# Attention scores as three fp32r products of high and low parts, with a new order of a turn's steps

## The chip, the cores and the metric

The kernel runs on one core of a Trainium2 chip. The metric is the device time of one execution in microseconds (us), the median of several runs. A core has five engines that run side by side, each through its own list of instructions in order: TensorE (PE, its weight loads shown as PEld), VectorE (DVE), ScalarE (ACT), GpSimd (POOL) and SyncE (SP, which issues most of the transfers). They wait for one another by semaphores. TensorE reads its operands from the on-chip memory SBUF and writes its results to PSUM, from where VectorE and ScalarE fetch them.

## The reference, cut to what matters

Attention over 8 batches of 8 heads, 576 tokens, 64 channels a head, with a mask by blocks of 64 tokens; then a mixture of 8 experts, of which each token takes one.

```python
def _attn_ref(q, k, v):
    scores = scale * np.matmul(q, k.transpose(0, 1, 3, 2))       # scale = 1/8
    mask = block_i >= block_j                                     # blocks of 64
    scores = np.where(mask, scores, -1000000000.0)
    scores = scores - np.max(scores, axis=-1, keepdims=True)
    attn = np.exp(scores)
    attn = attn / (np.sum(attn, axis=-1, keepdims=True) + 1e-09)
    return np.matmul(attn, v).astype(np.float32)

def _moe_ref(x, w_gate, w1, w2):
    expert_idx = np.argmax(x @ w_gate, axis=1)
    ...
        ye = np.maximum(xe @ w1[e], 0.0) @ w2[e]
        out[mask] = gate_w[mask, None] * ye
```

## The kernel before

**Two stages.** The attention with the router runs first, to about 380 us of the profile; the experts follow. Only the attention is touched. The experts' matmuls already work in fp32r, a float32 format that keeps a part of the mantissa: each factor is split into a high part and the rest, and three products (high by high, low by high, high by low) are summed in PSUM.

**Units.** Two heads make a unit m, 32 in all. The two heads' channels lie in the two halves of the 128 partitions, so a matmul on rows 0 to 63 is the first head's (tiles xa, ya), one on rows 64 to 127 the second's (xb, yb). The 576 queries are cut into a tile 0 of 64 rows and tiles 1 to 4 of 128 rows. Tile i meets 64 + 128 i keys.

**Steps of a unit.** The steps have names, and the number after a colon in the table ORDER is the lag: step X:3 in turn t works on unit t - 3.
- ld loads q (qd), k (kd) and v on SP's queue; pQ scales q by 1/8 (GpSimd, and VectorE for unit 0).
- S0 to S4 are the scores of the tiles, on TensorE: S0 one fp32 matmul of 128 rows for both heads, S1 (192 columns a head), S2 (320), S3 (448), S4 (2 x 288) one fp32 matmul a head on 64 rows. An fp32 matmul shows as two records in the profile.
- K sets the masked corner (VectorE), M takes the row maximum (VectorE), E the exp with its row sum (ScalarE); A and B are the two heads.
- T transposes exps (TensorE, four 128x128 at a time: Ta1, Ta2, Tb1, Tb2, Tk0, Tx3; Tt0 for tile 0), H copies the result to SBUF (@A ScalarE, @D VectorE), V0 to V5 multiply with v (TensorE, two heads in the two 64-column halves of the array), O and O0 copy the output to SBUF.
- F1, F2, F0 transpose the output and give the router's products (TensorE), X and Y scale them (VectorE) with R1 and R2 (one over the sums); Z scales tile 0 (GpSimd).
- z and y run one step of the router of a finished batch, or of what is postponed.

**What sets the order.** `run` goes through ORDER once a turn and issues each step, so ORDER alone fixes each engine's list. There is no planner at run time.

**Buffers.** The scores have two pairs of PSUM banks, "sa" and "sb": S4 (xa, xb) and S1 to S3 (ya, yb) of a unit, and then the next unit, take turns in them, so S4 of a unit waits for the exps E1 to E3 of the unit before, and S1 to S3 wait for E4. The transposes have two banks "pt" in turn. S0, V5 and F1 share a bank "o2", and F2 and F0 the next use of the same bank, so F2 waits for the readers of F1. The output of V has one bank "o".

Of the kernel before, what the change touches and what calls it, by code (L numbers as in the profile page):

```python
# [38 lines left out]
class Attention:  # L39
# [8 lines left out]
    def __init__(self, ctx, tc, ident, qT, kT, vt, w_gate, ends, po):  # L48
        self.tc, self.nc = tc, tc.nc
        self.qT, self.kT, self.vt = qT, kT, vt  # L50
        self.po = po

        self.ends = ends.rearrange("p (i c) -> p i c", c=P)
        self.M = qT.shape[0] * H // 2
        nc = self.nc
        cp = ctx.enter_context(tc.tile_pool(name="acst", bufs=1))
        self.raw = ctx.enter_context(tc.tile_pool(name="araw", bufs=3))
        self.rawv = ctx.enter_context(tc.tile_pool(name="arawv", bufs=5))
        self.spl = ctx.enter_context(tc.tile_pool(name="aspl", bufs=2))
# [32 lines left out]
    def op_ld(self, m):  # L92

        nc = self.nc
        b = m // 4
        qd = self.raw.tile([P, QS], F32, tag="qd", name=f"qd{m}")
        kd = self.raw.tile([P, S], F32, tag="kd", name=f"kd{m}")
        v = self.rawv.tile([P, VS, D], F32, tag="v", name=f"v{m}")
        nc.sync.dma_start(qd, self.qT[b, m % 4])
        nc.sync.dma_start(kd, self.kT[b, m % 4])  # L100
        nc.sync.dma_start(v, self.vt[b, m % 4])
        self.raws[m] = (qd, kd, v)

# [58 lines left out]
    def op_S(self, m, i):  # L162

        mm = self.nc.tensor.matmul
        q, k = self.qs[m], self.raws[m][1]
        if i == 0:
            mm(self.part(1, m, "S0", 432, 496), q[:, 512:], self.raws[m][0][:, 512 + P :], start=True, stop=True)  # L167
            return
        e = 64 + 128 * i
        for c in range(2 if i == 4 else 1):  # L170
            for j in range(2):
                out, _ = self.region(m, i, j)
                if i == 4:
                    out = out[:, c]
                n = out.shape[-1]
                o = (0 if j else S - e) + n * c
                r = slice(64 * j, 64 * j + 64)
                ins = mm(  # L178
                    out, q[r, 128 * (i - 1) : 128 * i], k[r, o : o + n], start=True, stop=True, skip_group_check=True
                )  # L180
                self.uses(m, i, j, ins)
# [187 lines left out]
    def run(self, order, sink, part, other, then, loaded):  # L369

        order = [(name, int(lag)) for name, lag in (x.split(":") for x in order.split())]
        last = max(lag for name, lag in order if name[0] not in "yz")
        left = [20] * (self.M // 4)
        more, pace, asks = iter(()), 1, None

        ends = {  # L380
            "F1": ("F2", "F0"), "X1": ("X2", "Y0@D"), "Y1": ("Y2",), "F2": ("F1",), "X2": ("X1",), "Y2": ("Y1",),
            "F0": (), "Y0@D": (),
        }
        for turn in range(self.M + last):
            if turn == self.M + last - 1:
                order = [(x, lag) for name, lag in order for x in ends.get(name, (name,))]
            for name, lag in order:
                m = turn - lag
                if name[0] == "z":
                    for _ in range(pace):  # L390
                        if asks is None:
                            asks = next(more, None)
                    continue
                if name[0] == "y":
                    other()
# [12 lines left out]
                if name[0] in "XY":
                    left[m // 4] -= 1
                    if left[m // 4] == 5:  # L410
                        part(m // 4, self.xs[m // 4][0])
                    if left[m // 4] == 0:
                        assert asks is None and next(more, "end") == "end"
                        (more, pace), asks = sink(m // 4, *self.xs.pop(m // 4)), None
        while asks != "end":
            if asks == "bank":
                next(then, None)
                asks = more.send(self.ps_t.tile([P, 512], F32, tag="pt", name="bank")[:, 0 : 6 * E])
            else:
# [12 lines left out]

# [889 lines left out]
```

## Time and profile before

| | |
|---|---|
| median of 3 runs | 861.1 us (860.74 to 861.51) |
| the profiled execution's own time | 863.59 us |
| its span, first to last instruction | 861.8 us |
| TensorE busy | 835.7 us (97%), mean granted clock 0.993 |
| ScalarE, VectorE, GpSimd busy over the span | 458.6, 397.9, 395.6 us |
| lines of the score products, busy | 58.3 us for ya, 58.3 us for yb, 41.6 us each for xa and xb, in pairs at the same time |

A row of the timeline gives start, duration, engine, line, operation, output <- inputs, shape and how many instructions were merged into the row (x4). A matmul's duration runs until its last result is in PSUM, so a matmul overlaps the next one; what one costs in a row of them is the distance of the starts. A row that starts after a change of the array's shape starts with its weight load. "[1.43 <-DVE neg L194]" is idle time of the engine before the row and who ended it.

### The profile page before, as it was taken

Reading aid. Unit: us, or ns where it says so; the run is one execution under the profiler, and the core shown is the slowest. Engines: PE = TensorE matmul, PEld = TensorE weight load, DVE = VectorE, ACT = ScalarE, POOL = GpSimd, SP = SyncE. Lnnn points to the kernel's source line nnn. Section 1 sums busy time; section 2 is a strip of 40 time slices with the busy share of each in tenths; the row PEclk is TensorE's granted clock in tenths of the full one; section 3 lists DMA queues with packets and bytes.
Section 4 is the critical chain, followed back from the end, with each engine's and each line's share of the span. In section 5 each row is a group of like instructions: output and inputs, shape, how many; then the busy total and the mean of one; then the engine's idle time right before and its main releaser. Section 6 shows DMA issues by size and latency. Waiting matters only on the chain.

```text
span 861.8 us, 15862 instructions
## 1 busy us (share of the span) xinstructions
PE 835.7 (97%) x4936; PEld 631.1 (73%) x4936; DVE 397.9 (46%) x1145; ACT 458.6 (53%) x1154; POOL 395.6 (46%) x389
## 2 busy tenths in 40 slices
PE   6999999999999999989999999999999999999993
PEld 4666666666666666657888888888888888888882
DVE  4667776777776777658505200047356451000000
ACT  5777777777777777724434443444344334433431
POOL 3222333333444624255845544456656565445451
PEclk9999999999999999999999999999999999999997
DMA  5234638363626355324713411045536431111110
GB/s 197 97 119 157 148 121 162 102 162 96 163 96 151 108 121 176 88 61 172 240 50 123 147 50 43 32 147 178 185 133 238 148 110 38 49 50 37 38 51 28
DMA packets 45687, 99.33 MB, mean 115 GB/s; under 512 B 7585, under 2 KB 10913, under 8 KB 45602
## 3 DMA queue, kind: packets, MB, share of 16 engines
q1 hardware_dynamic: 38082, 78.26, 31.0%
q0 software_dynamic: 7520, 19.97, 7.0%
q8 instruction: 49, 0.80, 0.4%
q14 instruction: 36, 0.29, 0.1%
HBM read 76.76 MB, written 21.98 MB: 115 GB/s over the span
## 4 chain that ended last, share of the span: by engine, by line
PE 93%; ACT 2%; issue 1%; DVE 1%; POOL 1%; another core or an unknown queue 0%; DMA 0%; POOLq 0%; DVEq 0%; ACTq 0%
PE py L987 24%; PE o L903 12%; PE ph L903 12%; PE o L279 11%; PE ya L178 6%; PE xa L178 4%; PE pt L947 4%; PE o L314 3%; PE px L862 2%; PE o L308 1%; ACT pb L209 1%; PE o L167 1%; DVE rc L691 0%; PE sb L1289 0%
## 5 line engine op out<-in xcount | busy, mean ns | idle before, releaser
L987 PE MATMUL py<-w,low 128*128 (+1 forms) x912 | 229.9, 401 | 0.2 <-issue 0.2
L987 PEld LDWEIGHTS py<-w,low 128*128 128x128 f32 x912 | 166.3, 189 | 33.9 <-issue 0.6
L108 POOL TENSOR_SCALAR q<-qd 128x640 f32<-128x640 f32 x31 | 56.1, 1811 | 188.6 <-PE o L167 108.2
L1111 DVE CAST w<-raw 128x1024 fp32r<-128x1024 f32 x60 | 49.4, 873 | 191.1 <-PE o L903 139.6
L967 POOL TENSOR_TENSOR low<-hf,low 128x512 fp32r<-128x512 f32 x72 | 100.5, 1396 | 34.9 <-ACT hf L961 34.9
L881 POOL TENSOR_TENSOR xl<-xf,xh 128x512 fp32r<-128x512 f32 x38 | 50.8, 1338 | 90.2 <-ACT xf L875 90.1
L1117 DVE TENSOR_TENSOR w<-raw,w 128x1024 fp32r<-128x1024 f32 x60 | 80.4, 1400 | 0.0
L957 ACT CAST low<-pt 128x512 fp32r<-128x512 f32 x76 | 45.7, 602 | 57.4 <-PE pt L947 56.1
L903 PE MATMUL o<-w,xh 128*128 x280 | 75.5, 392 | 0.0
L903 PE MATMUL ph<-w,xh 128*128 x280 | 75.4, 391 | 0.0
L209 ACT ACTIVATE pb<-ya,neg 128x320 f32<-128x320 f32 (+2 forms) x93 | 48.5, 525 | 45.5 <-DVE neg L194 45.4
L1010 POOL DMA_INDIRECT out<-y,idx x35 | 40.6, 1161 | 64.0 <-ACT y L1004 64.0
L939 ACT ACTIVATE h<-o 128x512 f32<-128x512 f32 x37 | 22.2, 599 | 74.1 <-PE o L903 74.1
L903 PEld LDWEIGHTS ph<-w,xh 128*128 128x128 f32 x280 | 52.6, 188 | 11.8
L903 PEld LDWEIGHTS o<-w,xh 128*128 128x128 f32 x280 | 52.6, 188 | 11.6
L1004 ACT ACTIVATE y<-py,xg 128x512 f32<-128x512 f32 x38 | 26.2, 689 | 64.3 <-PE py L987 64.3
L939 ACT ACTIVATE h<-ph 128x512 f32<-128x512 f32 x37 | 22.2, 600 | 71.7 <-PE ph L903 71.7
L178 PE MATMUL yb<-kd,q 64*128 64x192 f32 (+1 forms) x186 | 58.3, 447 | 0.0
L178 PE MATMUL ya<-kd,q 64*128 64x192 f32 (+1 forms) x186 | 58.3, 447 | 0.0
L698 POOL DMA_INDIRECT tab<-toks,posi x40 | 41.8, 1044 | 25.1 <-DVE run L665 12.8
L961 ACT COPY hf<-pt 128x512 f32<-128x512 f32 x76 | 46.3, 609 | 10.2 <-POOL low L967 9.2
L844 POOL DMA_INDIRECT xg<-xd,idx x37 | 44.5, 1202 | 10.8 <-POOL idx L840 10.6
(963 smaller groups left out, 1828.8 us busy)
## 6 DMA issues: line engine op xcount, KB each, us to landing
raw<-w SPq DMA_DIRECT2D x60, 512.0 KB, 5.2
qd<-qT SPq DMA_DIRECT2D x32, 352.0 KB
v<-vt SPq DMA_DIRECT2D x32, 352.0 KB
kd<-kT SPq DMA_DIRECT2D x32, 288.0 KB
xd<-xt SPq DMA_DIRECT2D x7, 1026.0 KB
xd<-xg SPq DMA_DIRECT2D x9, 256.5 KB
xg<-w SPq DMA_DIRECT2D x8, 256.0 KB
xd<-x SPq DMA_DIRECT2D x8, 128.0 KB
```

What stands on the lines that cost most here:

```text
L108: engine.tensor_scalar(q, self.raws[m][0][:, 0 : 512 + P], 0.125, None, ALU.mult)
L178: ins = mm(out, q[r, 128 * (i - 1) : 128 * i], k[r, o : o + n], start=True, stop=True, skip_group_check=True)
L209: ins = self.nc.scalar.activation(dst, src, AF.Exp, bias=self.neg[m][:, c : c + 1], scale=1.0, accum_out=self.sums[m][:, c : c + 1])
L279: self.nc.tensor.matmul(out[r], self.raws[m][2][:, slot], self.ph[m, bank][:, c0:c1], start=t in (0, 5), stop=t in (4, 5), skip_group_chec ...
L881: pool.tensor_sub(self.xl, self.xf, self.xh).then_inc(sem["xp"], 1)
L903: m = pe.matmul(self.ph[f], x[:, P * k : P * k + P], weights(k, f, part), start=start and k == 0, stop=stop and k == 3,)
L957: act.copy(self.hh[t % 2][:, f], self.pt[f]).then_inc(sem["ha"], 1)
L961: act.copy(self.hf, self.pt[f]).then_inc(sem["ha"], 1)
L967: engine.tensor_sub(self.hl[t % 2][:, f], self.hf, self.hh[t % 2][:, f]).then_inc(sem["hp"], 1)
L987: m = pe.matmul(self.py[t % 2], h[:, c // 4, P * (c % 4) : P * (c % 4) + P], wf[:, bass.ds(off + (base + 512 * c), 512)], start=n == 0, st ...
L1111: dve.tensor_copy(hi, raw[m % nr]).then_inc(sem["wh"], 1)
L1117: dve.tensor_sub(lo, raw[m % nr], hi).then_inc(sem["wd"], 1)
```

## The change

Tiles 1 to 4 of the scores are computed from a high part and the rest in fp32r. Four steps take the place of pQ: cQ and cK (ScalarE) write the high parts qh = q/8 and kh = k rounded to fp32r, lQ (VectorE) the rest ql = q/8 - qh, lK (GpSimd; VectorE for unit 0) the rest kl = k - kh; q0 (GpSimd) scales tile 0's queries, whose S0 stays in fp32. Each fp32 matmul of S1 to S4 becomes three fp32r matmuls, qh by kh, qh by kl and ql by kh, added up in PSUM, and each of the three runs for the two heads in turn. kd has a pool of its own with two buffers instead of three. ORDER is another one, and in the first turn of lag 3 S0, M0 and E0 of unit 0 come behind E1B.

```diff
+        self.rawk = ctx.enter_context(tc.tile_pool(name="arawk", bufs=2))
...
-        kd = self.raw.tile([P, S], F32, tag="kd", name=f"kd{m}")
+        kd = self.rawk.tile([P, S], F32, tag="kd", name=f"kd{m}")
...
-    def op_pQ(self, m):
-
-        q = self.qs[m] = self.spl.tile([P, 512 + P], F32, tag="q", name=f"q{m}")
+    def half(self, m, k, n, dt=F32R):
+        t = self.qs.setdefault(m, {})[k] = self.spl.tile([P, n], dt, tag=k, name=f"{k}{m}")
+        return t
+
+    def op_cQ(self, m):
+
+        self.nc.scalar.activation(self.half(m, "qh", 512), self.raws[m][0][:, 0:512], AF.Copy, scale=0.125)
+
+    def op_cK(self, m):
+        self.nc.scalar.copy(self.half(m, "kh", S), self.raws[m][1])
+
+    def op_lQ(self, m):
+        self.nc.vector.scalar_tensor_tensor(
+            self.half(m, "ql", 512), self.raws[m][0][:, 0:512], 0.125, self.qs[m]["qh"], ALU.mult, ALU.subtract
+        )
+
+    def op_lK(self, m):
         engine = self.nc.gpsimd if m else self.nc.vector
-        engine.tensor_scalar(q, self.raws[m][0][:, 0 : 512 + P], 0.125, None, ALU.mult)
+        engine.tensor_sub(self.half(m, "kl", S), self.raws[m][1], self.qs[m]["kh"])
+
+    def op_q0(self, m):
+
+        self.nc.gpsimd.tensor_scalar(self.half(m, "q0", P, F32), self.raws[m][0][:, 512 : 512 + P], 0.125, None, ALU.mult)
...
-            for j in range(2):
...
+            for n, (x, y) in enumerate((("qh", "kh"), ("qh", "kl"), ("ql", "kh"))):
+                for j in range(2):
...
+                    ins = mm(
+                        out, q[x][r, 128 * (i - 1) : 128 * i], q[y][r, o : o + w], start=n == 0, stop=n == 2,
+                        skip_group_check=True,
+                    )
...
+            if turn == first:
+
+                turns = [x for x in order if x[0] not in ("M0", "E0")]
+                n = turns.index(("E1B", turn)) + 1
+                turns[n:n] = [(x, turn) for x in ("S0", "M0", "E0")]
+            else:
+                turns = [x for x in order if x[0] != "S0" or turn > x[1]]
...
 ORDER = """
-E3B:3 V5:4 z2:0 O0@D:4 ld:0 Ta1:3 O@A:4 Ha1@A:3 S0:3 S4:2 z6:0 M0:3 Tb1:3 Tk0:3 pQ:1 K4B:2 E0:3 R1:3 K4A:2 z1:0 M4B:2
...
+E2A:3 M0:3 V4:4 M1B:3 ld:0 Ta2:3 M2B:3 z2:0 z3:0 E1A:3 z5:0 Ta1:3 O@D:4 E0:3 E2B:3 z6:0 E1B:3 Ha2@D:3 R1:3 cK:1 F1:4
...
```

What the new ORDER does to the engines' lists is shown at three places. The rows give line, operation, output <- inputs and columns; x2 merges equal rows. In the names xa, xb, ya, yb are the scores, pt the transposes, o the output of V, o21 and o22 the shared small bank (S0 reads qd, V5 reads h0 or v, F reads fold and oT), and a name's first number is the unit.

TensorE from the last transposes of a unit to the V matmuls, before (unit 4's V, unit 5's scores; L245 is Tt0, L178 the scores, L279 V0 and V2):

```order
L248 MATMUL pt4x3_849<-ident_68,pb4_683 128x128 x4
L245 MATMUL pt4t0_854<-ident_68,p04_684 64x128
L178 MATMUL ya5_858<-kd5_510,q5_674 128x192
L178 MATMUL yb5_860<-kd5_510,q5_674 128x192
L178 MATMUL ya5_858<-kd5_510,q5_674 128x320
L178 MATMUL yb5_860<-kd5_510,q5_674 128x320
L178 MATMUL ya5_858<-kd5_510,q5_674 128x448
L178 MATMUL yb5_860<-kd5_510,q5_674 128x448
L279 MATMUL o4_877<-ph4k0_828,v4_377 64x512 x2
```

TensorE around the same steps, after (unit 3's Tt0 and V0, then the first four of S3's six rows of unit 4):

```order
L266 MATMUL pt3t0_838<-ident_68,p03_676 64x128
L300 MATMUL o3_841<-ph3k0_829,v3_290 64x512 x2
L198 MATMUL ya4_848<-kh4_624,qh4_634 128x448
L198 MATMUL yb4_850<-kh4_624,qh4_634 128x448
L198 MATMUL ya4_848<-kl4_789,qh4_634 128x448
L198 MATMUL yb4_850<-kl4_789,qh4_634 128x448
```

and where the scores end, after (the last of S1, then S0, Tx3, Tb1, V5, V2, V3):

```order
L198 MATMUL ya4_848<-kh4_624,ql4_711 128x192
L198 MATMUL yb4_850<-kh4_624,ql4_711 128x192
L186 MATMUL o214_873<-qd4_436,q04_820 128x64
L269 MATMUL pt3x3_882<-ident_68,pb3_675 128x128 x4
L269 MATMUL pt3b1_887<-ident_68,pb3_675 128x128 x4
L300 MATMUL o214_873<-h01_135,v3_290 64x64 x2
L300 MATMUL o3_841<-ph3a2_781,v3_290 64x384
L300 MATMUL o3_841<-ph3b2_856,v3_290 64x384
L300 MATMUL o3_841<-ph3x3_898,v3_290 64x256 x2
```

V0 stands alone ahead of the scores, which run from S3 to S1 now, and S0 with two groups of transposes stands between them and the other V matmuls; before, all V matmuls followed the scores in one group, and S0 stood ahead of S4.

TensorE at the end of V and the start of S4, before (V4, V5, Ta1, S0, S4):

```order
L279 MATMUL o3_742<-ph3a2_714,v3_259 64x128
L279 MATMUL o3_742<-ph3b2_711,v3_259 64x128
L279 MATMUL o213_767<-h01_132,v3_259 64x64 x2
L248 MATMUL pt4a1_779<-ident_68,pb4_683 128x128 x4
L167 MATMUL o213_767<-qd4_375,q4_542 128x64
L178 MATMUL xa5_789<-kd5_510,q5_674 128x288
L178 MATMUL xb5_791<-kd5_510,q5_674 128x288
```

and after (V4, Ta2, Ta1, F1, the first rows of S4):

```order
L300 MATMUL o3_841<-ph3a2_781,v3_290 64x128
L300 MATMUL o3_841<-ph3b2_856,v3_290 64x128
L269 MATMUL pt4a2_924<-ident_68,pb4_835 128x128 x4
L269 MATMUL pt4a1_931<-ident_68,pb4_835 128x128 x4
L335 MATMUL o214_873<-fold_138,oT3_936 128x144 x2
L198 MATMUL xa5_956<-kh5_784,qh5_794 128x288
L198 MATMUL xb5_958<-kh5_784,qh5_794 128x288
L198 MATMUL xa5_956<-kl5_949,qh5_794 128x288
```

F1, which reads the copy oT of the bank that V4 ends, stands two groups behind V4 and ahead of S4; before, it stood behind S4, Tb1 and Tk0.

ScalarE from the exps of tiles 1 to 3 on, before (L209 exps, L286 O, L260 H):

```order
L209 ACTIVATE pb5_815,sums5_812<-ya5_858,neg5_813 128x320
L209 ACTIVATE pb5_815,sums5_812<-yb5_860,neg5_813 128x192
L209 ACTIVATE pb5_815,sums5_812<-ya5_858,neg5_813 128x448
L209 ACTIVATE pb5_815,sums5_812<-ya5_858,neg5_813 128x192
L209 ACTIVATE pb5_815,sums5_812<-yb5_860,neg5_813 128x320
L209 ACTIVATE pb5_815,sums5_812<-yb5_860,neg5_813 128x448
L286 COPY oT4_922<-o4_877 128x512
L260 COPY ph5a1_924<-pt5a1_917 128x512
```

and after (L281 H, L230 exps, L114 cK, L111 cQ):

```order
L281 COPY ph3x3_898<-pt3x3_882 128x512
L281 COPY ph3b1_904<-pt3b1_887 128x512
L230 ACTIVATE pb4_835,sums4_832<-ya4_848,neg4_833 128x448
L230 ACTIVATE pb4_835,sums4_832<-ya4_848,neg4_833 128x320
L230 ACTIVATE pb4_835,sums4_832<-ya4_848,neg4_833 128x192
L230 ACTIVATE p04_836,sums4_832<-o214_873,neg4_833 128x64
L230 ACTIVATE pb4_835,sums4_832<-yb4_850,neg4_833 128x320
L230 ACTIVATE pb4_835,sums4_832<-yb4_850,neg4_833 128x192
L114 CAST kh6_944<-kd6_758 128x576
L281 COPY ph4a1_951<-pt4a1_931 128x512
L111 ACTIVATE qh6_954<-qd6_757 128x512
```

O has left ScalarE for VectorE, cK and cQ have come, and Hx3 and Hb1 stand ahead of E3A, E2A, E1A, E0, E2B and E1B, the readers of the banks that S4 of the next unit writes.

## Rows read from the trace of the kernel before

**Rows 1.** Windows, attention: length, busy us of PE, PEld, DVE, ACT, POOL; clock, DMA.

```profile
25.36:349.62 324.26, 323.75 (x2392) 216.29 (x2392) 231.43 (x884) 242.98 (x734) 117.05 (x111) 1.00 0.49 132
```

**Rows 2.** Timeline, TensorE, one turn: start, us, engine, line, out<-in, columns, merged count.

```profile
58.67 0.51 PE L178 MATMUL xa<-kd,q 64*128 64x288 f32 x1
...
59.50 0.40 PE L178 MATMUL xa<-kd,q 64*128 64x288 f32 x1
...
60.33 0.60 PE L248 MATMUL pt4k<-ident,pb 128*128 128x128 f32 x4
60.77 0.66 PE L314 MATMUL o<-fold,oT 128*128 128x144 f32 x4
...
62.15 0.71 PE L314 MATMUL o<-fold,oT 128*128 128x144 f32 x4
62.79 0.46 PE L308 MATMUL o<-fold,oT 128*64 128x144 f32 x2
...
63.67 0.27 PE L245 MATMUL pt4t<-ident,p 128*64 128x128 f32 x1
...
64.84 0.54 PE L178 MATMUL ya<-kd,q 64*128 64x448 f32 x1
...
65.22 0.54 PE L178 MATMUL ya<-kd,q 64*128 64x448 f32 x1
...
66.60 0.49 PE L279 MATMUL o<-ph4a,v 128*64 128x384 f32 x1
...
69.73 0.51 PE L178 MATMUL xa<-kd,q 64*128 64x288 f32 x1
```

**Rows 3.** Timeline, TensorE's weight loads in the same turn.

```profile
58.67 0.18 PEld L178 LDWEIGHTS xa<-kd,q 64*128 64x128 f32 x1
58.67 0.18 PEld L178 LDWEIGHTS xb<-kd,q 64*128 64x128 f32 x1
58.78 0.19 PEld L178 LDWEIGHTS xa<-kd,q 64*128 64x128 f32 x1
...
63.98 0.19 PEld L178 LDWEIGHTS ya<-kd,q 64*128 64x128 f32 x1
```

**Rows 4.** Timeline, TensorE, the experts: first row of six groups of fp32r, and the row behind them.

```profile
434.02 1.08 PE L903 MATMUL ph<-w,xh 128*128 x4
...
439.52 0.60 PE L862 MATMUL px<-ident,xg 128*128 128x128 f32 x4
```

**Rows 5.** Timeline, ScalarE, the same turn.

```profile
60.53 0.59 ACT L260 COPY ph4b<-pt4b 128x512 f32<-128x512 f32 x1 [0.94 <-PE pt4b L248]
61.02 0.59 ACT L260 COPY ph4k<-pt4k 128x512 f32<-128x512 f32 x1
...
66.16 0.53 ACT L209 ACTIVATE pb<-ya,neg 128x320 f32<-128x320 f32 x1 [1.43 <-DVE neg L194]
...
69.25 0.60 ACT L286 COPY oT<-o 128x512 f32<-128x512 f32 x1
```

**Rows 6.** Timeline, VectorE's copy of 512 columns, and the last V4, O and F.

```profile
62.57 0.68 DVE L260 COPY ph4b<-pt4b 128x512 f32<-128x512 f32 x1
...
368.13 0.27 PE L279 MATMUL o<-ph31b,v 128*64 128x128 f32 x1
...
368.45 0.59 ACT L286 COPY oT<-o 128x512 f32<-128x512 f32 x1 [2.43 <-issue]
...
369.09 0.76 PE L314 MATMUL o<-fold,oT 128*128 128x144 f32 x4 [0.57 <-ACT oT L286]
```

**Rows 7.** Page, costliest groups: count, busy us, mean ns, idle before.

```profile
L108 POOL TENSOR_SCALAR q<-qd 128x640 f32<-128x640 f32 x31 | 56.1, 1811 | 188.6 <-PE o L167 108.2
...
L967 POOL TENSOR_TENSOR low<-hf,low 128x512 fp32r<-128x512 f32 x72 | 100.5, 1396 | 34.9 <-ACT hf L961 34.9
```

**Rows 8.** Timeline, the start.

```profile
3.85 0.77 DVE L108 TENSOR_SCALAR q<-qd 128x640 f32<-128x640 f32 x1 [2.24 <-DMA qd<-qT]
...
4.81 0.81 PE L178 MATMUL xa<-kd,q 64*128 64x288 f32 x1 [4.81 <-DVE fill L485]
```

More of the change, by code (lines that the diff above doesn't have):

```diff
@@ L164, in op_S @@
         mm = self.nc.tensor.matmul
-        q, k = self.qs[m], self.raws[m][1]
+        q = self.qs[m]
         if i == 0:
-            mm(self.part(1, m, "S0", 432, 496), q[:, 512:], self.raws[m][0][:, 512 + P :], start=True, stop=True)
+            mm(self.part(1, m, "S0", 432, 496), q["q0"], self.raws[m][0][:, 512 + P :], start=True, stop=True)
             return
@@ L170, in op_S @@
         for c in range(2 if i == 4 else 1):
-            for j in range(2):
[L172 to L181, printed above, removed]
+            for n, (x, y) in enumerate((("qh", "kh"), ("qh", "kl"), ("ql", "kh"))):
+                for j in range(2):
+                    out, _ = self.region(m, i, j)
+                    if i == 4:
+                        out = out[:, c]
+                    w = out.shape[-1]
+                    o = (0 if j else S - e) + w * c
+                    r = slice(64 * j, 64 * j + 64)
+                    ins = mm(
+                        out, q[x][r, 128 * (i - 1) : 128 * i], q[y][r, o : o + w], start=n == 0, stop=n == 2,
+                        skip_group_check=True,
+                    )
+                    self.uses(m, i, j, ins)
     def op_K(self, m, i, j):
@@ L341, in step @@
         k = name[0]
-        if name in ("ld", "pQ", "R1", "R2", "Z"):
+        if name in ("ld", "cQ", "cK", "lQ", "lK", "q0", "R1", "R2", "Z"):
             getattr(self, "op_" + name)(m)
@@ L378, in run @@
         more, pace, asks = iter(()), 1, None
+        first = dict(order)["E1B"]
         ends = {
@@ L384, in run @@
         for turn in range(self.M + last):
+            if turn == first:
[4 more added lines that the diff above has]
+                turns = [x for x in order if x[0] != "S0" or turn > x[1]]
             if turn == self.M + last - 1:
-                order = [(x, lag) for name, lag in order for x in ends.get(name, (name,))]
-            for name, lag in order:
+                turns = [(x, lag) for name, lag in order for x in ends.get(name, (name,))]
+            for name, lag in turns:
                 m = turn - lag
@@ L425 @@
 ORDER = """
-E3B:3 V5:4 z2:0 O0@D:4 ld:0 Ta1:3 O@A:4 Ha1@A:3 S0:3 S4:2 z6:0 M0:3 Tb1:3 Tk0:3 pQ:1 K4B:2 E0:3 R1:3 K4A:2 z1:0 M4B:2
-R2:3 F1:4 Hb1@A:3 Ta2:3 Hk0@A:3 X1:4 Y1:4 M4A:2 Tb2:3 F2:4 E4B:2 y0:0 Z:3 Hb2@D:3 F0:4 Ha2@A:3 Y2:4 z4:0 Tx3:3 Tt0:3
-E4A:2 X2:4 S1:2 z5:0 z0:0 z3:0 Ht0@A:3 Y0@D:4 S2:2 K1A:2 K2A:2 S3:2 K1B:2 Hx3@A:3 K2B:2 V0:3 V2:3 M2A:2 K3A:2 M1B:2
-M3A:2 E2A:2 E1B:2 V1:3 y1:0 E3A:2 V3:3 M1A:2 K3B:2 M2B:2 E1A:2 M3B:2 V4:3 E2B:2
+E2A:3 M0:3 V4:4 M1B:3 ld:0 Ta2:3 M2B:3 z2:0 z3:0 E1A:3 z5:0 Ta1:3 O@D:4 E0:3 E2B:3 z6:0 E1B:3 Ha2@D:3 R1:3 cK:1 F1:4
+X1:4 lK:2 Ha1@A:3 Y1:4 cQ:1 S4:2 Tk0:3 z1:0 Tb2:3 q0:2 y0:0 R2:3 F2:4 K4A:2 F0:4 Z:3 Hk0@A:3 K4B:2 M4A:2 Tt0:3 M4B:2
+V0:3 X2:4 E4A:2 Y0@D:4 E4B:2 z4:0 S3:2 Hb2@A:3 Y2:4 S2:2 S1:2 lQ:1 S0:2 z0:0 K3B:2 K3A:2 M3B:2 K1A:2 K2A:2 M3A:2 M1A:2
+Tx3:3 Tb1:3 Ht0@A:3 M2A:2 y1:0 V5:3 E3B:2 K1B:2 Hx3@A:3 V2:3 O0@D:3 Hb1@A:3 V3:3 E3A:2 V1:3 K2B:2
 """
```

## The prediction

> **What bounds the kernel now.** I read the page first, where TensorE is the one engine that is busy nearly throughout, then the view by windows for the attention part [rows 1]: between the first S4 matmul of unit 2 and that of unit 31, 29 turns, TensorE is busy in 323.75 of 324.26 us, ScalarE in 242.98 and VectorE in 231.43, at a granted clock of 1.00. A turn is 324.26/29 = 11.18 us, and one without extra router work 69.73 - 58.67 = 11.06 [rows 2]. So TensorE's own list of work sets the turn; the other engines have 8.38 (ScalarE), 7.98 (VectorE) and 4.04 us (GpSimd) of work in it. The expert stage after it isn't touched. Only what shortens TensorE's list, and no wait in its place, will move the end.
>
> "Busy" hides dead time, though. In the timeline of one turn [rows 2] the columns stream back to back inside a group, but between groups that use the array in different shapes (full, 64-row halves for S, 64-column halves for V and F0) nothing streams for a while. S4's last pair starts at 59.50 and takes 0.24, so it ends at 59.74; the transposes behind it take 0.109 each (four in 60.77 - 60.33) and must have begun at 59.90, since the next group starts at 60.33: **0.16 us dead**. Tt0 (one transpose, 63.67) ends at 63.78, the first S1 columns run at 63.98, when the first weights are in and the next load begins [rows 3]: **0.20**. S3 ends at 65.22 + 0.38 = 65.60, and V0, two times 0.43 before 66.60, begins at 65.74: **0.14**. Seven such changes stand in a turn.
>
> **The products.** An fp32 matmul is two records, each 0.83 ns a column: S4 4 x 0.24 (59.50 - 58.78 is three of them), S1 and S2 64.84 - 63.98 = 0.86, S3 2 x 0.38: 2.58 us a unit for both heads, which run side by side [rows 2, 3]. After it there are three fp32r matmuls in place of two records, 15 pairs instead of 10. The only fp32r rate in the trace is that of the experts: 24 matmuls of 512 columns from 434.02 to 439.52 [rows 4], 0.229 us each. That is 0.016 over the 0.213 that 512 columns would take at half of a record's 0.83 ns, and one size doesn't tell whether the excess grows with the columns. A pair can't follow the last sooner than a weight load: 58.78 - 58.67 = 0.11, the two halves at once [rows 3].
> - Excess by column (0.447 ns): S1 3 x 0.11, S2 3 x 0.143, S3 3 x 0.200, S4 6 x 0.129 = 2.13; gain 0.45.
> - Excess fixed at 0.016: 0.33 + 3 x 0.149 + 3 x 0.203 + 6 x 0.136 = 2.21; gain 0.37.
> - No excess: 0.33 + 3 x 0.135 + 3 x 0.187 + 6 x 0.12 = 2.02; gain 0.56.
>
> I take 0.41, between the first two, because both keep to the one row there is. 64-row fp32r isn't in the trace at all; the bound above is that the halves don't overlap (a rival below).
>
> The Trainium skill (TensorE: Matmul & The Clock Gate, Back-to-back issue gap) gives N/2.4 + 2.5 ns for a warm matmul, 216 ns at 512 columns. The experts' rows differ, with 229, so the rows stand in the sum; by the page the gain would be near the third line, a rival below.
>
> **The new order's changes of shape.** This is the part that speaks against it. V0 moves out of the V group to before S3, and S0 with two transposes comes between S1 and V5. Where a turn had Tt0|S1 and S3|V0 (0.20 + 0.14 = 0.34) it has Tt0|V0 (0.15, like S3|V0), V0|S3 (0.20), S1|S0 (0.20, since a 128-column load stands open as at Tt0|S1) and Tb1|V5 (0.15): 0.70. The others change their neighbours, not their kind; F0|Tt0 in place of F0|Tx3 loads half the weights and gives 0.03 back. Nine changes instead of seven, **+0.33 us**, between 0.28 and 0.37. So four fifths of what the products give go here.
>
> **Waits.** In this turn F2 should begin at 62.15 and, counted back from F0 at 62.79 (a gap of 0.20 less the load of 0.11, and four records of 144 columns, 0.12 each), begins at 62.22: it waits 0.07 for VectorE's X1 and Y1, which stand right behind F1. Now S4, Tk0 and Tb2 stand between F1 and F2, so that goes: -0.07, a little more in turns like those that make the mean 11.18. In its place F1 stands close behind V4: V4 ends, VectorE's copy O starts 0.21 later, takes 0.68 as a copy of 512 columns does there, the load comes 0.05 after it and takes 0.11: 1.05 us [rows 6]. Meanwhile TensorE does a change (0.16), Ta2 and Ta1 (0.87): 1.03. So F1 waits +0.02; 0 to 0.1. What next is late is S4, which needs the exps of the unit before out of its banks (third rival).
>
> **What lies beside.** ScalarE gets cQ and cK (a 512-column copy starts 61.02 - 60.53 = 0.49 after another there [rows 5], so 0.49 + 0.55) and gives O (0.47) away: 8.38 to 8.95. VectorE gets lQ and O (0.68 each): 7.98 to 9.34. GpSimd gives pQ away (1.81) for lK (1.396 x 576/512 = 1.57) and q0 (128 of pQ's 640 columns, 0.36) [rows 7]: 4.04 to 4.16. All lie under TensorE's 10.9, and cost nothing as long as that holds; VectorE is now at 85%, which is where the cover is thinnest. kd has two buffers instead of three: its load waits on SP's queue until lK has read the unit two before, with the v load and the router's row transfers queued behind it. Its reader cK comes a turn later, some 10 us, so 0.
>
> **Start and end.** The first S4 begins at 4.81, after VectorE's pQ at 3.85 [rows 8]. Now cK and cQ must run on ScalarE, then lQ and lK on VectorE before the second product: 0.55 + 0.49 + 0.68 + 0.76 = 2.5 from 3.85 to 4.8, so the second product comes at 6.3 to 7.3. S streams less in that stretch too. I put +1.0, between 0 and +2. The drain keeps its length: 0.
>
> **Sum.** -0.41 + 0.33 - 0.07 + 0.02 = -0.13 us a turn, 30 turns: -3.9; with the start -2.9. The profiled execution took 863.59 for its span of 861.8, 2.5 more than the runs' median 861.1; on it the sum gives 860.7, on the median **858.2 us**. With the ends of the gain (0.37, 0.45) and of the changes, 855 to 859.4.
>
> **Rivals.**
> - *The products run at full rate*: gain 0.56, 0.15 x 30 = 4.4 less, **853.8**. For it: fp32 records of the same shape show no excess (0.24 for 288 columns is 0.83 ns each). Against: every fp32r row has it. 0.11.
> - *The changes eat it all*: gain 0.37, changes 0.37, F1 waits 0.10: -0.37 + 0.37 - 0.07 + 0.10 = +0.03 a turn, +0.9, and the start between 0 and +1: **862**. It takes only the upper end of three terms, none of them far. 0.22.
> - *Slower: S4 waits for ScalarE.* S4 writes the banks that the exps of the unit before read. From the end of Tb1, ScalarE needs 0.20 to its copy (in the rows Tb1 ends at 60.33, its copy starts at 60.53), 0.49 for Hb1, then E3A, E2A, E1A, E2B, E1B (six exps take 69.25 - 66.16 = 3.09, less one of 448 columns, about 0.61: 2.48 [rows 5]), E0 taken as 0.49 and 0.05 to TensorE: 3.71. TensorE has in between, by columns at 0.83 ns and two records, V5 0.11, V2 0.64, V3 0.43, V1 0.85, V4 0.21, then Ta2 and Ta1 0.87, F1 0.48, and changes of 0.15, 0.16 and 0.09: 3.99. It decides from 0.28 more on ScalarE's chain, one maximum of VectorE that comes late; each 0.1 beyond costs 3.0 us. At 0.54 more: -0.13 + 0.26 = +0.13 a turn, +3.9 + 1.0, **866**. For it: ScalarE already starts its exps only after 1.43 us of idling for a maximum [rows 5], and VectorE gets 17% more work. 0.22.
> - *The halves don't run side by side in fp32r*, so the change doesn't do what it says: some 2 x 2.1 = 4.2 instead of 2.17, +2.0 x 30 on the forecast, **919**. Against: the fp32 halves load their weights in the same 0.11 [rows 3]. 0.03.
>
> **How the numbers follow.** The forecast has 0.42. A difference under 0.2% (1.7 us, 859.4 to 862.8) is about what a measurement of this kernel can tell from none. Faster: 0.42 + 0.11 = 0.53; same 0.22; slower 0.22 + 0.03 = 0.25. The likeliest's own range is 855 to 859.4. From 851.5 to 866 the range holds all of the forecast, the second case, most of the first and half of the third: about 0.84.
>
> **What would show it.** Right: pairs of 288 columns 0.13 apart, 448 0.20, 192 0.11; nine gaps of 0.15 to 0.20 in a turn; turns of 10.93; no idle time before S4. Wrong: pairs 0.12 apart (first rival); turns of 11.05 to 11.1 with the gaps larger or F1 waiting 0.1 (second); TensorE waiting before S4 for ScalarE's exps, or before a V matmul for its copy (third); the second half of a pair starting when the first ends (fourth).

## The result, and the profile after

The changed kernel takes **867.97 us** (median of 7 runs, 866.55 to 869.24) against 861.49 for the kernel before (7 runs, 860.74 to 864.37): ratio **1.0074**, 95% interval 1.0064 to 1.0085. It is slower by 6.5 us. The forecast was 858.2, and its range ended at 866. What follows is read from one profiled execution of each kernel. That of the kernel before took 2.5 us more than the median of its runs, that of the changed one 1.3 more, so the spans differ by 5.5 where the medians differ by 6.5.

The page of the changed kernel, head and busy times (engine, busy us, share, instructions). TensorE has 2.6 us less work than before and VectorE 51 us more, in a span that is 5.5 us longer:

```profile
span 867.3 us, 16704 instructions
## 1 busy us (share of the span) xinstructions
PE 833.1 (96%) x5256; PEld 644.7 (74%) x5256; DVE 449.3 (52%) x1209; ACT 471.3 (54%) x1186; POOL 402.4 (46%) x421
```

The view by windows of the changed kernel, first S4 matmul of unit 2 to that of unit 31, answers to [rows 1]: 327.34 us instead of 324.26, and TensorE idles 5.9 of them instead of 0.5.

```profile
core 0: us, PE busy (x) PEld busy (x) DVE busy (x) ACT busy (x) POOL busy (x), PEclk, DMA share, GB/s
27.90:355.24 327.34, 321.46 (x2688) 227.24 (x2688) 276.43 (x942) 254.11 (x762) 124.85 (x140) 1.00 0.48 128
```

Three stretches make up the 5.5: S4 of unit 2 starts 2.54 later (27.90 against 25.36), the 29 turns take 3.08 more, and from S4 of unit 31 to the end there is 0.12 less.

The products run as forecast. TensorE's timeline of the changed kernel at an undisturbed S4 and at the start of the next: from the second pair on, pairs of 288 columns follow each other at 0.13, both halves at once.

```profile
231.18 0.40 PE L198 MATMUL xa<-kh,qh 64*128 64x288 f32 x1
...
231.42 0.29 PE L198 MATMUL xa<-kl,qh 64*128 64x288 f32 x1
231.43 0.29 PE L198 MATMUL xb<-kl,qh 64*128 64x288 f32 x1
231.56 0.29 PE L198 MATMUL xa<-kh,ql 64*128 64x288 f32 x1
231.69 0.29 PE L198 MATMUL xa<-kh,qh 64*128 64x288 f32 x1
...
242.16 0.39 PE L198 MATMUL xa<-kh,qh 64*128 64x288 f32 x1
```

From 231.18 to 242.16 are 10.98; the turns without router work take 10.96 to 10.98, called a **clean turn of 10.97** here (11.06 before, 10.93 forecast). But in most batches of four units one turn takes 11.4, and in four of them the next takes 12.2 to 12.5. They are turns with the router's work. TensorE's waits of the changed kernel in that stretch, as far as they are longer than the 0.15 that the view counts (waiting instruction <- what released it: us in all, times, longest), are of these three kinds; the third stands four times, once in each of the four long turns:

```profile
PE o L335 <- ACT pb L230: 2.2, 6, 0.7
PE o L186 <- PE yb L198: 2.1, 4, 0.8
PE o L300 <- ACT ph17x L281: 0.4, 1, 0.4
```

**The long turn.** VectorE and GpSimd of the changed kernel, in the turn whose S4 starts at 207.66:

```profile
211.01 0.29 DVE L351 COPY x<-o 64x144 f32<-64x144 f32 x1
211.22 2.77 DVE L623 TENSOR_TENSOR oh<-cd,w 128x40 bf16<-128x40 f32 x1
213.91 0.18 DVE L354 TENSOR_TENSOR lg<-o,rs 128x32 f32<-128x32 f32 x1
214.01 0.67 DVE L117 SCALAR_TENSOR_TENSOR ql<-qd,qh 128x512 fp32r<-128x512 f32 x1
214.70 0.11 DVE L210 MEMSET yb<- 64x64 f32 x1
...
210.75 1.43 POOL L123 TENSOR_TENSOR kl<-kd,kh 128x576 fp32r<-128x576 f32 x1
212.13 0.56 POOL L127 TENSOR_SCALAR q<-qd 128x128 f32<-128x128 f32 x1
212.63 1.29 POOL L1267 TENSOR_TENSOR high<-xg,zero 128x512 fp32r<-128x512 f32 x1
```

The router's step oh has 40 columns, and takes 0.18 and 0.20 in the two batches where GpSimd idles beside it. Here it takes 2.77: it ends when GpSimd has finished lK, q0 and the weight split. In three batches it takes 2.44 to 2.46 (the same three steps). In the last two, without a split behind q0, it takes 0.70 and 0.71, and ends 0.07 behind lK, while q0 still runs. What stands behind it on VectorE is late: Y2, for which S0 waits (for the bank), and ql, then the maxima of S3, for which ScalarE waits, and then V3 for ScalarE's copy:

```profile
215.50 0.63 ACT L230 ACTIVATE pb<-yb,neg 128x448 f32<-128x448 f32 x1 [3.50 <-DVE neg L215]
...
214.19 0.41 PE L186 MATMUL o<-qd,q 128*128 128x64 f32 x2 [0.77 <-PE yb L198]
...
216.76 0.65 PE L300 MATMUL o<-ph17x,v 128*64 128x256 f32 x4 [0.36 <-ACT ph17x L281]
```

The Trainium skill (SBUF — State Buffer, "SBUF: two separate sides") says that VectorE and GpSimd share one pair of SBUF ports as an exclusive lock: a VectorE step with two SBUF inputs and a GpSimd step that reads SBUF don't run at once. The trace agrees in that oh takes 0.70 instead of 0.18 and ends right behind lK; that it was not let in between the three steps, here and in three other batches, goes beyond what is said there.

**The turn ahead of it.** VectorE and TensorE of the changed kernel, in the turn before (S4 at 196.24). VectorE's ql takes 1.56, as lK runs beside it until 200.91, and from there to O VectorE has no pause. At the end three router steps (z2, z3, z5) stand ahead of O. V4 ends at 205.5, O starts at 206.17, and F1 waits.

```profile
199.89 1.56 DVE L117 SCALAR_TENSOR_TENSOR ql<-qd,qh 128x512 fp32r<-128x512 f32 x1
...
201.64 0.11 DVE L210 MEMSET yb<- 64x64 f32 x1
...
205.10 0.61 DVE L607 TENSOR_REDUCE L<-lg 128x32 f32<-128x256 f32 x1
205.82 0.20 DVE L610 TENSOR_REDUCE m<-L 128x5 f32<-128x40 f32 x1
206.05 0.20 DVE L612 TENSOR_TENSOR L<-L,m 128x40 f32<-128x40 f32 x1
206.17 0.68 DVE L307 COPY oT<-o 128x512 f32<-128x512 f32 x1
...
207.00 0.73 PE L335 MATMUL o<-fold,oT 128*128 128x144 f32 x4 [0.31 <-ACT pb L230]
```

The view names ScalarE's pb as what released F1, but that had long been done; what came last is O (206.17 + 0.68 = 206.85, and the load). In all five turns of this kind (11.41 to 11.43) ql takes 1.56. How much is the hold of ql and how much the three steps, b_z4_lq tells below.

### The profile page after: what moved, and what is told of

Read it like the earlier page. It is cut to its first block, busy times and chain, and to the rows that moved or that the text cites. A ratio compares the mean times of both kernels' runs of the same rounds, so it can differ in the third digit from the quotient of the medians.

```text
span 867.3 us, 16704 instructions
## 1 busy us (share of the span) xinstructions
PE 833.1 (96%) x5256; PEld 644.7 (74%) x5256; DVE 449.3 (52%) x1209; ACT 471.3 (54%) x1186; POOL 402.4 (46%) x421
## 4 chain that ended last, share of the span: by engine, by line
PE 87%; DVE 5%; ACT 4%; issue 2%; DMA 0%; POOL 0%; SPq 0%; POOLq 0%; DVEq 0%; ACTq 0%
PE py L1016 25%; PE ph L932 12%; PE o L932 12%; PE o L300 9%; PE o L335 4%; PE pt L976 4%; PE ya L198 4%; PE xa L198 3%; ACT pb L230 2%; PE px L891 2%; DVE neg L215 2%; PE o L329 1%; DVE ql L117 1%; PE o L186 1%; DVE oh L623 1%
## 5 line engine op out<-in xcount | busy, mean ns | idle before, releaser
L1140 DVE CAST w<-raw 128x1024 fp32r<-128x1024 f32 x60 | 47.4, 841 | 189.0 <-PE o L932 136.3
L243 POOL TENSOR_SCALAR p<-p,rs 128x64 f32<-128x64 f32 x32 | 14.1, 442 | 199.1 <-DVE rs L239 138.0
L1146 DVE TENSOR_TENSOR w<-raw,w 128x1024 fp32r<-128x1024 f32 x60 | 83.8, 1454 | 0.0
L230 ACT ACTIVATE pb<-yb,neg 128x448 f32<-128x448 f32 (+2 forms) x93 | 49.7, 550 | 57.6 <-DVE neg L215 53.9
L932 PEld LDWEIGHTS ph<-w,xh 128*128 128x128 f32 x280 | 52.6, 188 | 11.8
L727 POOL DMA_INDIRECT tab<-toks,posi x40 | 43.6, 1089 | 32.3 <-DVE lg L354 13.3
L230 ACT ACTIVATE pb<-ya,neg 128x448 f32<-128x448 f32 (+2 forms) x93 | 48.4, 544 | 0.0
L335 PE MATMUL o<-fold,oT 128*128 128x144 f32 x256 | 44.4, 296 | 3.5 <-ACT pb L230 2.2
```

The costliest lines, as they stand in the source:

```text
L230: ins = self.nc.scalar.activation(dst, src, AF.Exp, bias=self.neg[m][:, c : c + 1], scale=1.0, accum_out=self.sums[m][:, c : c + 1])
L335: mm(t[:, i], self.oT[m, 0][:, o : o + P], w, start=True, stop=True)
L932: m = pe.matmul(self.ph[f], x[:, P * k : P * k + P], weights(k, f, part), start=start and k == 0, stop=stop and k == 3,)
L1140: dve.tensor_copy(hi, raw[m % nr]).then_inc(sem["wh"], 1)
L1146: dve.tensor_sub(lo, raw[m % nr], hi).then_inc(sem["wd"], 1)
```

## Experiments

**Theory**: the change cuts TensorE's list as forecast, but GpSimd's new steps lK and q0 lie beside VectorE's, and each holds the other (stretches it while it runs). **Rivals**: VectorE simply has too much work in the router's turns; or the products or the order cost more than read.

Starts of S4, from TensorE's timeline of each profiled execution (29 turns from S4 of unit 2 to that of unit 31; the next column is the rest of the span), and medians beside the kernel before on the same chip:

| kernel | S4 of unit 2 | clean turn | 29 turns | last S4 to end | median us | ratio to before (95%) |
|---|---|---|---|---|---|---|
| before | 25.36 | 11.06 | 324.26 | 512.2 | 861.5 | 1 |
| changed | 27.90 | 10.97 | 327.34 | 512.1 | 868.0 | 1.0064 to 1.0085 |
| a_z4 | 28.34 | 10.97 | 325.77 | 511.0 | 866.6 | 1.0051 to 1.0119 |
| b_z4_lq | 28.89 | 10.97 | 322.22 | 510.7 | 863.7 | 1.0018 to 1.0053 |
| c_z2 | 28.38 | 10.97 | 326.65 | 511.9 | 868.8 | 1.0053 to 1.0149 |
| d_turn | 26.32 | 10.64 | 319.33 | 509.3 | 856.3 | 0.9923 to 0.9956 |
| i_order | 26.33 | 11.41 | 332.89 | 509.4 | 870.3 | 1.0089 to 1.0123 |
| h_v0 | 30.91 | 11.48 | 334.99 | 516.5 | 877.0 | 1.0169 to 1.0203 |
| f_y0 | 25.79 | 10.63 | 311.75 | 514.0 | 853.4 | 0.9893 to 0.9927 |
| g_y0_y1 | 25.76 | 10.63 | 319.70 | 514.9 | 861.9 | 0.9999 to 1.0019 |
| k_drain | 26.49 | 10.63 | 311.83 | 509.6 | **849.5** | 0.9846 to 0.9879 |

**a_z4: the router step oh earlier.**

```diff
-S4:2 Tk0:3 z1:0 Tb2:3
+S4:2 Tk0:3 z1:0 z4:0 Tb2:3
...
-E4B:2 z4:0 S3:2
+E4B:2 S3:2
```

> One step of the order is moved: z4 (in the turns with 12.2 to 12.5 us it issues VectorE's router step oh) stands right behind z1, two us before GpSimd starts lK. Theory: a VectorE step from SBUF to SBUF is held as long as GpSimd works. Then oh takes 0.20 instead of 2.5 to 2.8, S0 no longer waits 0.8 for its bank, but the next SBUF step in the list, ql, is now the one that is held to the end of GpSimd's row lK, q0, weight split, so K3B comes at most 0.5 earlier and V3's wait grows from 0.4: the long turns fall to 11.7 to 12.2 and the whole by 1 to 3, 865 to 867. Rival: oh waits for data of its own, or VectorE simply has too much work in these turns: oh is as long in the new place or nothing else gets shorter; 868, 12.2 to 12.5 a turn.

Measured: 866.6, oh is 0.20 in all eight batches, S0 waits nowhere. And, as the theory had it, ql is held in its place: 1.2 to 2.5 in 18 of the last 23 turns, where it takes 0.67 alone. VectorE and GpSimd of a_z4 in the turn that answers to the one above:

```profile
210.93 0.17 DVE L354 TENSOR_TENSOR lg<-o,rs 128x32 f32<-128x32 f32 x1
211.03 1.53 DVE L117 SCALAR_TENSOR_TENSOR ql<-qd,qh 128x512 fp32r<-128x512 f32 x1
...
210.61 1.41 POOL L123 TENSOR_TENSOR kl<-kd,kh 128x576 fp32r<-128x576 f32 x1
211.99 0.97 POOL L127 TENSOR_SCALAR q<-qd 128x128 f32<-128x128 f32 x1
```

lK ends at 212.02, and ql 0.54 later; q0, which takes 0.53 alone, is now held by ql. The time is in the range given, and its lead over the changed kernel (1.3) is no more than the spread of its runs; its spread over the turns isn't as forecast: the long ones fell to 11.1, but the turn two ahead of each grew from 10.97 to 11.5 or 11.7, with ql at 2.3 to 2.5 there.

**b_z4_lq: ql out of the way of lK too**, on a_z4.

```diff
-M4B:2 V0:3 X2:4
+M4B:2 lQ:1 V0:3 X2:4
...
-S1:2 lQ:1 S0:2
+S1:2 S0:2
```

> z4 behind z1 as before and also lQ (VectorE's step ql) right behind M4B, ahead of GpSimd's lK, so that no SBUF to SBUF step of VectorE stands beside lK, q0 and the weight split. Theory (held by GpSimd): oh 0.20, ql 0.67 in every turn, the waits of S0 (0.8) and V3 (0.4) go, turns of 12.2 to 12.5 fall to 11.0 to 11.3; six batches, 4 x 1.1 + 2 x 0.3 = 5 us less, 863. Rival (too much work for VectorE in these turns): the list holds the same work, so 867 to 868.

Measured: 863.7, 4.3 below the changed kernel. No turn takes 12 any more; those of 11.4 and 12.2 are 11.1 to 11.2 (two near the end stay at 11.8 and 11.3, as in the changed kernel). VectorE has the same steps to do, so too much work is not the cause: where they stand beside GpSimd's is. TensorE idles 1.1 us in the 29 turns of b_z4_lq:

```profile
28.89:351.11 322.22, 321.10 (x2690) 227.62 (x2689) 271.79 (x942) 255.12 (x762) 130.42 (x141) 1.00 0.49 130
```

One part of the forecast fell: ql isn't 0.67 in every turn. It takes up to 1.19, beside a weight split or lK, and lK or q0 is held by it in turn; but VectorE still idles ahead of the maxima in those turns, so nothing waits for that. In six turns a step of 8 columns (run) is held instead, 1.83 to 1.85 for 0.15, and they take 11.09 instead of 10.97. VectorE of b_z4_lq in the turn that answers to the one of 11.41 above (S4 at 194.85):

```profile
197.47 0.68 DVE L117 SCALAR_TENSOR_TENSOR ql<-qd,qh 128x512 fp32r<-128x512 f32 x1
...
200.02 0.11 DVE L210 MEMSET yb<- 64x64 f32 x1 [1.02 <-PE yb L198]
```

The maxima begin 5.17 behind S4, as in a clean turn, instead of 5.40, and the turn is 11.18 instead of 11.41, with z2, z3 and z5 ahead of O as before. So of the 0.44 over a clean turn some 0.23 was the hold of ql, and 0.21 are what the three steps cost.

**c_z2: the long router step away from O.**

```diff
-M2B:3 z2:0 z3:0 E1A:3
+M2B:3 z3:0 E1A:3
...
-S0:2 z0:0 K3B:2
+S0:2 z0:0 z2:0 K3B:2
```

> Only z2 (the router step of 0.61 us that stands on VectorE between the last maxima and the copy O in the turn before the long one) is moved behind z0, some 4 us earlier, into a stretch where VectorE idles. Theory: the turns of 11.41 us are longer by 0.43 because F1 waits for O behind that step; they fall to 10.97 to 11.05, six of them, 2.5 us less in all: 865.4. Rival: F1 waits for O because of something else (ScalarE's exps, the bank): 11.4 and 868.

Measured: 868.8, no gain, and the turns of 11.41 fell to 11.31 only. F1's wait went (O starts 206.12, 0.2 behind V4), but not because O came early: it starts 9.82 behind S4 instead of 9.93, and V4 ends later. The stretch in which VectorE was to idle is where ql is held, as in the changed kernel. VectorE of c_z2, a turn before:

```profile
199.96 1.56 DVE L117 SCALAR_TENSOR_TENSOR ql<-qd,qh 128x512 fp32r<-128x512 f32 x1
201.45 0.26 DVE L601 TENSOR_REDUCE L<-x 64x8 f32<-64x64 f32 x1
201.63 0.60 DVE L607 TENSOR_REDUCE L<-lg 128x32 f32<-128x256 f32 x1
202.25 0.11 DVE L210 MEMSET yb<- 64x64 f32 x1
```

The maxima come 0.6 later, and V3 begins 8.01 after S4 instead of 7.75. VectorE's steps follow each other without a pause from ql to O, so a step moved inside that row wins next to nothing. That F1 waits for O stands; that the place of z2 is what makes O late fell.

**d_turn: the products alone, in the order of the kernel before.**

```diff
-... M0:3 Tb1:3 Tk0:3 pQ:1 K4B:2 E0:3 R1:3 ...
+... M0:3 Tb1:3 Tk0:3 K4B:2 E0:3 cQ:1 R1:3 ...
...
-Y0@D:4 S2:2 K1A:2 K2A:2 S3:2 K1B:2 Hx3@A:3 K2B:2
+Y0@D:4 lQ:1 S2:2 K1A:2 K2A:2 S3:2 K1B:2 Hx3@A:3 cK:1 lK:1 q0:1 K2B:2
```

> The three fp32r products in the turn's order of the kernel before (seven changes of shape, O on ScalarE, S0 after the exps), with cQ behind E0, cK, lK and q0 behind Hx3, lQ behind Y0. Theory: the products are worth the forecast 0.41 a turn and the new order costs 0.33 of it, so clean turns are 11.06 - 0.41 = 10.65 (0.32 shorter than 10.97), and with the start 1 to 2.5 later the whole comes to 861.5 - 12.3 + (1 to 2.5) = 850 to 852. Rival: the old order has no room for ScalarE's two more steps, and a wait for its exps or copies takes the place: turns of 10.97 or more, 860 or more.

Measured: **856.3**, faster than both. Clean turns are 10.64, so the products are worth 0.42 a turn, and the new order costs 10.97 - 10.64 = 0.33 of it. kd has its two buffers here too, so they are not what makes the changed kernel slower. The 4 to 6 us that are missing from the 850 to 852 are in ten turns of 11.28 to 11.81 (7.2 over 10.64 together), where VectorE's copy O0 starts 0.91 to 1.13 behind the last matmul of V5 instead of 0.27, and S0 waits for it. VectorE, GpSimd and TensorE of d_turn in two of them:

```profile
188.62 0.22 DVE L311 COPY oT<-o 128x64 f32<-128x64 f32 x1 [0.88 <-PE pt16a L269]
...
187.88 0.97 POOL L719 DMA_INDIRECT tab<-toks,posi  x1 [0.30 <-issue]
...
188.90 0.43 PE L186 MATMUL o<-qd,q 128*128 128x64 f32 x2 [0.42 <-issue]
...
221.27 1.22 DVE L667 COPY xt<-g 128x4 f32<-128x4 f32 x1
222.40 0.21 DVE L311 COPY oT<-o 128x64 f32<-128x64 f32 x1
...
221.19 1.27 POOL L1259 TENSOR_TENSOR high<-xg,zero 128x512 fp32r<-128x512 f32 x1
```

In the first a scatter of GpSimd began 0.2 behind V5; in the second a copy of 4 columns, 0.16 elsewhere, takes 1.22 beside a weight split, and O0 queues behind it.

**i_order: the order alone**, with the fp32 scores of the kernel before.

```diff
-... R1:3 cK:1 F1:4 X1:4 lK:2 Ha1@A:3 Y1:4 cQ:1 S4:2 ... Tb2:3 q0:2 y0:0 ... S1:2 lQ:1 S0:2 ...
+... R1:3 F1:4 X1:4 pQ:1 Ha1@A:3 Y1:4 S4:2 ... Tb2:3 y0:0 ... S1:2 S0:2 ...
```

> The other half alone: the new order with the fp32 scores of the kernel before (pQ on GpSimd where lK stands; no cQ, cK, lQ). Theory: the order costs 0.33 for its two more changes of shape and gives the wait of F2 back, so clean turns are 10.97 + 0.41 = 11.38; its start is about 1.5 later (S4 of unit 2 at 26.9), and turns with router work still wait where GpSimd's pQ and a split stand in a row: 872 to 877. Rival (the order in itself is free and only its combination with the new products is slow): turns of 11.06 to 11.1, 861 to 864.

Measured: 870.3, outside what either gave; the clean turns are as the theory had them, 11.41, that is 0.35 over 11.06. TensorE waits nowhere by as much as the view counts, and no turn of the 29 but one is over 11.61. pQ starts later in the turn than lK did, oh is 0.18 to 0.20 in all eight batches, and the long turns of 872 to 877 don't arise.

**h_v0: two changes of shape undone**, on b_z4_lq.

```diff
-lQ:1 V0:3 X2:4 ... y1:0 V5:3 E3B:2
+lQ:1 X2:4 ... y1:0 V5:3 V0:3 E3B:2
```

> The changed kernel with z4 and lQ moved as in b_z4_lq (863.7, clean turns 10.97) and V0 moved from before S3 to behind V5, where it has the shape of its neighbours. That undoes two changes of shape: Tt0|V0, V0|S3 and Tb1|V5 stay as Tt0|S3 and Tb1|V5. Theory (each change costs 0.15 to 0.20 whatever stands beside it): clean turns of 10.97 - 0.15 = 10.82, 29 of them, 4.4 less: 859.3. Rival (the 0.33 of the new order is something else, or V0 there covered a wait of S3 or of the V products): clean turns of 10.95 or more, 863 to 865.

Measured: 877.0, clean turns 11.48. The theory fell, and the rival is right in its kind (V0 covered a wait of S3) but not in its size: 877 is far over its 863 to 865. The profiled execution took 884.2, so only its turns are read here. ScalarE and TensorE of h_v0 behind Tt0, and its longest kind of wait:

```profile
68.25 0.74 ACT L230 ACTIVATE pb<-xb,neg 128x576 f32<-128x576 f32 x1
...
69.13 0.47 PE L198 MATMUL yb<-kh,qh 64*128 64x448 f32 x1 [0.18 <-ACT pb L230]
...
PE yb L198 <- ACT pb L230: 5.7, 28, 0.3
```

xb and yb are the same two banks (one tag, one buffer), so S3 waits for the exp of tile 4, which in the new order ends late. One half then runs behind the other, and the group takes 2.0 instead of 1.35 from its first product to its last. In the changed kernel V0 stands there and covers that. So its two changes of shape stand in for a wait on the late exps.

**f_y0: GpSimd's router step behind Z**, on d_turn.

```diff
-E4B:2 y0:0 Z:3 Hb2@D:3
+E4B:2 Z:3 y0:0 Hb2@D:3
```

> The three products in the old order (run d_turn, 856.3) with one step moved: y0, which gives GpSimd a router scatter or a weight split, stands behind Z instead of before it, so that it runs at some 3 us into a turn and not at the turn's end. In d_turn ten turns of 11.3 us have VectorE's copy O0 start 0.92 to 0.95 behind V5 instead of 0.27, with a scatter begun 0.2 behind V5, and S0 waits 0.4 to 0.5 for it. Theory (GpSimd's work on SBUF holds VectorE): O0 is at 0.27 everywhere, the waits of S0 (4.3 in all) go, 852 to 853. Rival (O0 waits for something else, or the scatter only stands beside it): O0 as late as before, 856.

Measured: 853.4, just over what the theory gave. O0 starts 0.27 behind V5 in every turn, the 29 turns take 311.75 instead of 319.33. Of these 7.6 the end took 4.7 back: at the end of the last turn O0 met five scatters in a row. VectorE, TensorE and windows of f_y0:

```profile
358.02 0.23 DVE L311 COPY oT<-o 128x64 f32<-128x64 f32 x1 [4.37 <-remote]
...
358.39 0.73 PE L335 MATMUL o<-fold,oT 128*128 128x144 f32 x4 [2.12 <-DVE oT L311]
...
357.00:373.00 16.00, 12.67 (x60) 9.54 (x61) 6.41 (x26) 3.08 (x8) 4.49 (x6) 0.79 0.15 40
359.03:365.86 6.83, 5.94 (x19) 4.48 (x19) 3.01 (x13) 1.31 (x3) 1.98 (x3) 0.50 0.11 22
```

TensorE idled 2.12 up to 358.39, and from 359.03 to 365.86 the granted clock is 0.50, its lower level (1.2 GHz).

**g_y0_y1: y1 behind Z as well.**

```diff
-Z:3 y0:0 Hb2@D:3 ... V1:3 y1:0 E3A:2
+Z:3 y0:0 y1:0 Hb2@D:3 ... V1:3 E3A:2
```

> As f_y0, and y1 too stands behind Z: both of GpSimd's router or weight steps run 3 to 5.5 us into a turn. Theory: nothing of GpSimd is left beside O0, M0 and R1, but VectorE's router steps and lQ (some 4.5 to 6.3 us into a turn) may now be held by up to 1 us in the turns with two splits, ahead of the score tiles' maxima: 851.5 to 854, at best 1 below f_y0, at worst 1 above it. Rival: where GpSimd's steps stand makes no difference, 856.

Measured: 861.9, outside what either gave. Ten turns are 11.2 to 11.8 and one 13.05, with TensorE waiting for exps before Ta1 and once 0.5 for lK itself; the one of 13.05 also has a granted clock of 0.51 from 290.6 to 294.1. That two steps of GpSimd in a row hold more behind them than one at a time would fit; which step of VectorE is held in each of these turns I didn't trace, so it isn't shown.

**k_drain: O0 of the last turn on ScalarE**, on f_y0.

```diff
+            "O0@D": ("O0@A",),
```

> As f_y0 (853.4), with one copy changed: in the last turn O0 of unit 31 is on ScalarE instead of VectorE. In f_y0 that one copy started 1.97 behind V5, among five scatters of GpSimd in a row, TensorE waited 2.1 for it, and the granted clock of the 16 us around it was 0.79; the time from the last S4 to the end was 514.0 against 509.3 in d_turn. Theory (a copy of VectorE held by GpSimd's scatters): ScalarE isn't held, F0 starts 2 us earlier, the clock stays at 1.00, from the last S4 to the end 509 to 510, 848.5 to 850. Rival (the drain is longer because the turns before it are shorter and the gathers come late, whoever copies): 513 to 514 from the last S4, 853 to 854.

Measured: **849.5**, ratio 0.9863 (0.9846 to 0.9879), and 509.6 from the last S4 to the end. The window of k_drain that answers to the last one above has the clock at 1.00:

```profile
358.40:374.40 16.00, 14.63 (x79) 11.10 (x78) 11.18 (x33) 4.09 (x8) 8.51 (x8) 1.00 0.18 34
```

F2 starts 1.08 behind the start of V5 instead of 2.41, 1.3 earlier, but the end comes 4.4 earlier (509.6 instead of 514.0). The other 3.1 are lost behind F2 in f_y0, most of them in the 6.8 us at the lower clock: the first group of four matmuls of 512 columns behind F2 takes 1.88 there and 1.03 in k_drain.

## Why the prediction was wrong

- **What bounds the kernel, and the products**: right. The gain of 0.41 a turn was 0.42 (d_turn against before), the pairs stand 0.13 apart, the halves run side by side. The first and the fourth rival fell.
- **Changes of shape and the waits of F1 and F2**: the forecast for the order was 0.33 - 0.07 + 0.02 = 0.28 a turn; measured 0.33 (changed against d_turn) and 0.35 (i_order against before). Too low by about 0.06, 1.7 us in all. The step here was right and its size a little small. That these are nine gaps of the given sizes wasn't measured one by one; h_v0, meant for that, met a wait instead.
- **What lies beside**: here it failed, with the largest term. "All lie under TensorE's 10.9, and cost nothing as long as that holds" is a sum of busy times, and VectorE was rightly called the thinnest cover. But what it lacked wasn't time. lK and q0 replaced one step of GpSimd by two at another place in the turn, beside VectorE's oh and ql, and z2, z3, z5 stood ahead of an O that was ScalarE's before. Over 29 turns of 10.97, 318.1 us, the changed kernel lost 9.2; over 29 of 11.06 the kernel before lost 3.5. The difference, 5.7, was costed at nothing. b_z4_lq loses 4.1 over 318.1 with the same work in another order, so 5.1 of the 5.7 are the places of oh and ql beside lK, q0 and the splits.
- **The third rival** (S4 waits for ScalarE's exps) would have given 866, close to what came, but that is luck: TensorE doesn't wait at S4 by as much as the view counts. The rival that was missing is one engine holding another. The second rival fell too: clean turns are 10.97, not 11.05 to 11.1.
- **The start**: +1.0 forecast, +2.54 measured. Only the products were priced there; they alone cost 0.96 (d_turn), near the forecast, and the order alone 0.97 (i_order). That the order moves S0 and the transposes of the first turns was not costed at all. The 0.6 that is left is no more than the start differs between kernels whose first turns are nearly alike (27.90 to 28.89, and 25.76 to 26.49), and stays open.
- **The drain**: 0 forecast, -0.12 measured in the profiled executions, as far as these tell (see the medians above).
- **The range of the likeliest case**: with the ends of the gain and of the changes together the sum is -0.22 to -0.05 a turn, 855.5 to 860.6, not 855 to 859.4. 868.0 lies outside either.

In sum, beside the forecast's -2.9: -2.6 by the clean turns (29 x -0.09; the forecast's -0.13 makes -3.8), +5.7 by holds and, for a small part, the steps ahead of O, +2.5 by the start, -0.1 at the end: +5.5, as the span shows.

## What to carry to other kernels

A step on an idle engine is priced not by its busy time alone, but also by which other engine it holds while it runs: list what VectorE reads from SBUF beside each long step of GpSimd, and who waits for that. Put GpSimd's long steps where nobody waits for the VectorE step beside them; in b_z4_lq ql is still held in many turns, and costs nothing there. One moved entry of the order was worth 3 us here (f_y0). And where a change has two parts, try each alone: the products without the new order are faster than the kernel before, and the order gives back four fifths of their gain before any wait.

## What the runs showed of the hardware

- A VectorE step with two inputs from SBUF was stretched to the end of a computing step of GpSimd: 40 columns (oh) in 0.18 alone, 0.70 to the end of lK, 2.44 to 2.77 to the end of lK, q0 and a split; 512 columns (ql) in 0.67 alone, 1.56 beside lK. A copy of 4 columns from SBUF to SBUF went from 0.16 to 1.22 beside a split (d_turn).
- It goes both ways: lK takes 1.41 to 1.43, and 1.85 to 1.88 where ql came first (b_z4_lq); q0 0.53, and 0.97 beside ql (a_z4).
- GpSimd's steps in a row needn't let VectorE in between: oh missed two such seams at 212.13 and 212.63 in the changed kernel, while it got in behind lK in two other batches, and ql in a_z4 got in at one. What decides that stays open.
- A copy out of PSUM (O0) started on time, 0.27 behind V5, beside weight splits in d_turn, but nine times 0.91 to 0.98 behind it, beside a scatter that had begun 0.04 to 0.06 before the copy was due; it then started 0.70 to 0.77 behind the scatter's start, before the scatter's end. Once (at 111.11) it was on time beside such a scatter. Why is open; that the scatter is the cause is shown by f_y0, where it was moved and the copy is on time. On ScalarE the one such copy (k_drain) was on time, 0.27, beside a scatter.
- In f_y0 the granted clock was 0.50 (1.2 GHz) for 6.8 us after TensorE had idled for 2.12; in k_drain, with 0.80 of idling at the same place, it stayed at 1.00.
